# A new hand-listed order of the pinned stretch, with five chunks of batch 0 mixed in plain fp32 in place of three

## The chip, the cores and the metric

The kernel runs on one core of one Trainium2 chip. The metric is device microseconds (us) of one execution; the kernel before took 568.13 us, the median of three runs between 565.83 and 570.65. The profile shows one further execution.

## The reference, cut to what matters

Three layers run one after the other on 4 batches of 768 tokens with 384 channels (8 heads of 48):

```
state = alpha[t] * state + outer(k[t], v[t]);  y[t] = q[t] @ state          # gated linear attention, per head
theta = x @ w_theta;  zr = x*cos(theta);  zi = x*sin(theta)
y = w_tok_r @ zr + w_tok_i @ zi                                             # mix over all 768 tokens
u = x + y;  u = u + relu(u @ w_ch)
h = relu(u @ w_in);  c = conv3 over tokens(h);  out = (h * sigmoid(c)) @ w_out
```

All values are float32. The weights arrive as 64-bit words from which the kernel puts together the float32 numbers itself.

## The kernel before, in words

A *chunk* is 128 tokens; chunk numbers 0 to 23 run over four batches of six. For a chunk the attention part does this, each step under the name that the order list uses:

- `load`: SyncE (SP) fetches alpha (`a_t`), q and k (`qk_t`) and v. `hl` does it for the theta weights, `wl` for the twelve pieces of the token-mixing weights.
- `back`, `fore`, `mul`: VectorE (DVE) forms products of decays by a scan in either direction (L315, L329) and multiplies q and k by them (L344).
- `kps`, `sc`: TensorE (PE) transposes k (L364) and forms the scores; `pt0`, `pt1`: ScalarE (ACT) copies the scores' two halves out of PSUM (L379), and GpSimd (POOL) zeroes what lies above the diagonal (L380). `kt` is ACT's copy of the transposed k (L391).
- `y`, `kv`: PE multiplies the masked scores by v, adds q times the state that the chunk before left, and forms this chunk's addition to the state. `st`: DVE adds it (L446), and POOL multiplies by the decay in two instructions (L448). The next chunk's `y` needs both of them and both masks.
- `x`, `xt`, `u`: ACT copies y out, PE transposes it (L461), and ACT copies it to `u` (L466).

Then the second layer begins: `th` (PE, x times the theta weights `whole`), `int`, `frac`, `abs`, `sin` (ACT and DVE bring the angle into range and take sine and cosine), and `zm` (DVE, L514). For most chunks the product is split into a rounded high part (`tc`, ACT, L523) and a low rest (`tl`, DVE, L529), and `m0`, `m1`, `m2` mix it with the token weights, split in the same way (`lc` on ACT, L223; `ll` on DVE, L230), in three passes of the fast format: high by high, high by low, low by high. For the chunks listed in `PLAINS`, which exist in batch 0 alone, nothing is split: `zm` writes the operand and PE multiplies in plain fp32, which the profile records as two instructions for each matmul (`yps<-full,zh`). The two halves of the output tokens have a piece of token weights each, so an index of `m` is half times 6 plus chunk. `wo` decodes one piece of token weights on DVE in three instructions (L154, L155, L156), `wh` the theta weights, in a part of 768 columns and one of 384, each followed by a scaling on ACT (L288).

All of this for the chunks 0 to 13 and for the whole mixing of batch 0 stands in one string, `ORDER`. Its tokens are run from left to right, and `in_order` (L604) chains the instructions of each compute engine in just this sequence, so no engine can take a later instruction of the string while an earlier one waits. SP is not chained, but a later load waits behind an earlier one in its queue. `warm.n` puts in n matmuls on constants whose result nothing uses. Behind the string come the mixing of batches 1 to 3 and the last layer, where a scheduler sets the order. The token weights of the `PLAINS` chunks are split for the later batches: for the first half by `lc` and `ll` in the string, for the second half inside the loop over batch 1 if the string has not done it. The last chunk of `PLAINS` gets its low part by way of another buffer and one more copy on ACT (L234).

Of the kernel before, what the change touches and what calls it, by code (L numbers as in the profile page):

```python
# [37 lines left out]
STB = 2  # L38
NWARM = 13
WHOLE = 2  # L40
PLAINS = (0, 1, 3)
FINEY = 0
FINEK = 2 * NC
EARLY = 99
AHEAD = 2
ORDER = (
# [25 lines left out]
)  # L72
ENGINES = (mybir.EngineType.PE, mybir.EngineType.DVE, mybir.EngineType.Activation, mybir.EngineType.Pool)
MAGIC = 12582912.0
# [5 lines left out]
def tile_gated_linear_attention__then__spectral_moe__then__conv_gate(  # L80
# [53 lines left out]
    def body(top, slow):  # L134
# [50 lines left out]
        with ExitStack() as ph1:  # L185
# [12 lines left out]
            def tok_tile(h, dtype, name):  # L198
                return tok_ps[h].tile([P, 2, HALF], dtype, tag="w", name=name, bufs=2 * NC)


            def load_tok(h, c):
# [8 lines left out]
                nc.sync.dma_start(out=st[:, : 2 * n].bitcast(U32).rearrange("p (a n) -> p a n", a=2), in_=src)  # L211
                if c in PLAINS:
                    w = tok_tile(h, F32, "full").rearrange("p i t -> p (i t)")
# [11 lines left out]
            def tok_low(h, c):  # L225
                if slow:
                    return
                last = PLAINS and c == PLAINS[-1]
                lo = zf_p.tile([P, 2, DM], F32R, tag="zf", name="wlow") if last else tok_tile(h, F32R, "wtok")
# [240 lines left out]
            def t_mm(ci):  # L470
                b, c = divmod(ci, NC)
                xt = ub[b][:, :, c * P : (c + 1) * P]
                plain = ci in PLAINS and not slow
                zh = z_p.tile([P, 2, DM], F32 if plain else F32R, tag="zh", name="zh", bufs=ZH)
# [35 lines left out]
            def t_mul(ci):  # L510
                zh, th, z = ths[ci]
                plain = ci in PLAINS and not slow
                x = xs.pop(ci)
# [6 lines left out]
            def t_cast(ci):  # L520
                zh, th, z = ths[ci]
                if ci not in PLAINS or slow:
                    nc.scalar.copy(zh, z)  # L523

            def t_low(ci):
                zh, th, z = ths.pop(ci)
                if ci not in PLAINS or slow:
                    zl = z_p.tile([P, 2, DM], F32R, tag="zl", name="zl", bufs=NC)
# [418 lines left out]
```

## Time and profile before

| | |
|---|---|
| median of three runs | 568.13 us (565.83 to 570.65) |
| the profiled execution | 569.6 us, of which 567.9 us lie between the first and the last instruction |
| PE busy | 548.5 us (97%) |
| DVE busy | 451.2 us (79%) |
| ACT busy | 334.0 us (59%) |
| POOL busy | 90.9 us (16%) |
| mean granted TensorE clock | 0.989 of 2.4 GHz |

Matmuls overlap, and each one's record lasts longer than the pitch at which they follow each other. What PE needs for a run of equal matmuls is therefore read from start to start. PE counts as busy while a `warm` matmul runs, too, so that the busy share of the first stretch says little.

### The profile page before, as it was taken

How to read it: one execution, taken by the hardware profiler on the slowest of the kernel's cores; microseconds unless marked ns; L12 is line 12 of the kernel's file. 1: busy time of each engine (PE TensorE's matmuls, PEld its weight loads, DVE VectorE, ACT ScalarE, POOL GpSimd, SP SyncE). 2: the span in 40 equal slices, each digit the busy share in tenths (PEclk: the TensorE clock that was granted, in tenths of full speed). 3: DMA queues.
4: the chain of work that ended last, by engine and by line, in shares of the span. 5: the costliest groups of instructions: out<-in, count | busy, mean ns of one | idle time of the engine just before them, and what ended most of it. 6: DMA issues, size and time to landing. Idle time of an engine off the chain costs nothing.

```text
span 567.9 us, 13255 instructions
## 1 busy us (share of the span) xinstructions
PE 548.5 (97%) x5550; PEld 497.5 (88%) x5551; DVE 451.2 (79%) x680; ACT 334.0 (59%) x682; POOL 90.9 (16%) x99
## 2 busy tenths in 40 slices
PE   7879999999999999999999997999999999999996
PEld 4556778677998999899999996799999999999996
DVE  7995999999968775534757989887888888898780
ACT  4655673658736676435632436567667766676671
POOL 2573363333314102430000000000000000000000
PEclk9998999999999999999999999999999999999999
DMA  8664556553224301300024335200154342646001
GB/s 324 194 192 143 184 145 235 148 213 90 71 72 141 127 1 48 110 18 0 1 83 165 85 98 180 87 6 36 25 186 139 126 160 105 204 141 240 17 29 47
DMA packets 24995, 65.56 MB, mean 115 GB/s; under 512 B 2528, under 2 KB 8672, under 8 KB 24544
## 3 DMA queue, kind: packets, MB, share of 16 engines
q1 hardware_dynamic: 24928, 64.64, 34.6%
q8 instruction: 45, 0.74, 0.6%
q14 instruction: 22, 0.18, 0.1%
HBM read 59.92 MB, written 4.72 MB: 114 GB/s over the span
## 4 chain that ended last, share of the span: by engine, by line
PE 79%; DVE 11%; DMA 6%; POOL 2%; issue 1%; ACT 1%; SPq 0%; DVEq 0%; POOLq 0%
PE yps L99 22%; PE ops L99 18%; PE hps L99 16%; PE th L99 6%; PE y L99 5%; PE sc L99 4%; PE cps L99 3%; DMA stage<-in_w_out_dram 2%; PE kv L99 2%; DMA stage<-in_w_in_dram 2%; DVE stage L155 2%; PE xps L461 1%; DMA stage<-in_w_theta_dram 1%; DVE stage L156 1%; PE kps L364 1%
## 5 line engine op out<-in xcount | busy, mean ns | idle before, releaser
L99 PE MATMUL yps<-wtok,zh 128*128 128x384 f32 x504 | 133.7, 340 | 0.0
L99 PE MATMUL hps<-x,win 128*128 128x386 f32 x576 | 108.3, 340 | 0.0
L99 PE MATMUL ops<-wout,g 128*128 128x384 f32 x576 | 107.0, 337 | 0.0
L99 PEld LDWEIGHTS hps<-x,win 128*128 128x128 f32 x576 | 103.0, 190 | 0.5
L99 PEld LDWEIGHTS ops<-wout,g 128*128 128x128 f32 x576 | 101.6, 188 | 0.5
L99 PEld LDWEIGHTS yps<-wtok,zh 128*128 128x128 f32 x504 | 90.8, 188 | 2.4 <-ACT zh L523 0.3
L99 PE MATMUL yps<-wtok,zl 128*128 128x384 f32 x252 | 84.4, 335 | 0.0
L380 POOL TENSOR_SCALAR_AFFINE_SELECT pt<-pt 128x512 f32<-128x512 f32 x48 | 51.5, 1087 | 107.8 <-ACT pt L379 107.3
L99 PEld LDWEIGHTS yps<-wtok,zl 128*128 128x128 f32 x252 | 47.3, 188 | 0.1
L108 DVE TENSOR_TENSOR g<-cv,g 128x384 fp32r<-128x384 f32 x64 | 35.4, 555 | 12.1 <-ACT g L107 11.1
L99 PE MATMUL cps<-us,wch 128*128 128x512 f32 x162 | 41.3, 404 | 3.6 <-DVE u L714 1.9
L771 ACT ACTIVATE cv<-cv 128x384 f32<-128x384 f32 x64 | 33.1, 522 | 19.9 <-DVE cv L768 19.8
L772 DVE SCALAR_TENSOR_TENSOR cv<-cv,hh 128x384 f32<-128x384 f32 x64 | 35.2, 555 | 10.4 <-ACT cv L771 8.9
L315 DVE TENSOR_TENSOR_SCAN fbt<-a_t,onehot 128x516 f32<-128x516 f32 x24 | 30.3, 1261 | 14.6 <-ACT a_t L336 12.9
L765 DVE SCALAR_TENSOR_TENSOR cv<-hh,cw,cv 128x383 f32<-128x383 f32 (+1 forms) x64 | 38.8, 615 | 3.3 <-ACT cv L762 2.8
L762 ACT ACTIVATE cv<-hh,cw 128x384 f32<-128x384 f32 x64 | 38.6, 614 | 4.0 <-DVE g L108 3.8
L107 ACT CAST g<-cv 128x384 fp32r<-128x384 f32 x64 | 32.6, 510 | 13.3 <-DVE cv L772 12.0
L99 PEld LDWEIGHTS cps<-us,wch 128*128 128x128 f32 x162 | 30.6, 191 | 11.2 <-DVE u L714 2.4
L768 DVE SCALAR_TENSOR_TENSOR cv<-hh,cw,cv 128x384 f32<-128x384 f32 (+1 forms) x64 | 38.8, 615 | 1.0
L379 ACT COPY pt<-sc 128x512 f32<-128x512 f32 x48 | 26.8, 589 | 19.6 <-PE sc L99 11.3
L760 ACT ACTIVATE hh<-hps 128x386 f32<-128x386 f32 x64 | 31.5, 492 | 9.5 <-PE hps L99 9.3
L448 POOL TENSOR_TENSOR S<-tst,ftot 48x192 f32<-48x192 f32 x32 | 31.0, 969 | 37.2 <-DVE tst L446 30.9
(101 smaller groups left out, 847.9 us busy)
## 6 DMA issues: line engine op xcount, KB each, us to landing
qk_t<-in_qka_dram SPq DMA_DIRECT2D x24, 512.0 KB, 4.2
stage<-in_w_tok_dram SPq DMA_DIRECT2D x12, 768.0 KB, 4.7
top<-in_w_tok_dram SPq DMA_DIRECT2D x12, 768.0 KB, 4.4
a_t<-in_qka_dram SPq DMA_DIRECT2D x24, 260.0 KB, 2.8
v_t<-in_v_dram SPq DMA_DIRECT2D x24, 192.0 KB, 4.2
out_dram<-ob SPq DMA_DIRECT2D x24, 192.0 KB, 1.9
stage<-in_w_in_dram SPq DMA_DIRECT2D x4, 768.0 KB, 5.1
stage<-in_w_out_dram SPq DMA_DIRECT2D x4, 768.0 KB, 5.2
```

The lines of the kernel that those rows point to most:

```text
L99: nc.tensor.matmul(o, lhsT, rhs, start=start, stop=stop, skip_group_check=True)
L107: cast = nc.scalar.copy(hi, src)
L108: lo_eng.tensor_tensor(lo, src, hi.bitcast(F32), ALU.subtract)
L315: nc.vector.tensor_tensor_scan(bf[:, AW:0:-1], at[:, AW:0:-1], of[:, AW:0:-1], 0.0, ALU.mult, ALU.add)
L380: nc.gpsimd.affine_select(pt, pt, [[0, NP], [1, P]], ALU.is_ge, 0.0, base=0, channel_multiplier=-1)
L448: nc.gpsimd.tensor_tensor(Sn[r, :, e], tt[r, :, e], nft[r].unsqueeze(2).to_broadcast([D, NP, D]), ALU.mult)
L760: nc.scalar.activation(hh, ps[:, :HW], AF.Relu)
L762: nc.scalar.activation(cv, hh[:, o : o + HALF], AF.Copy, scale=cw[:, f, 1:2])
L765: nc.vector.scalar_tensor_tensor(cv[:, a:HALF], hh[:, o + a - 1 : o + HALF - 1], cw[:, f, 0:1], cv[:, a:HALF], ALU.mult, ALU.add)
L768: nc.vector.scalar_tensor_tensor(cv[:, 0:e], hh[:, o + 1 : o + 1 + e], cw[:, f, 2:3], cv[:, 0:e], ALU.mult, ALU.add)
L771: nc.scalar.activation(cv, cv, AF.Tanh, scale=0.5)
L772: nc.vector.scalar_tensor_tensor(cv, cv, 1.0, hh[:, o : o + HALF], ALU.add, ALU.mult)
```

## The change: five plain chunks and another order

`PLAINS` takes in five chunks of batch 0. The plain chunks need no `tc` and no `tl`, their mixing takes two recorded instructions for each plain matmul in place of three fast passes, and with chunk 4 as the last of the list, its low weights take the detour that chunk 3's took. In the string `ORDER` all tokens but a few stand elsewhere; the second half's weights are split in the string for chunk 5 alone and for the other five in the loop over batch 1. The number of `warm` matmuls goes from 35 to 33.

```diff
-PLAINS = (0, 1, 3)
+PLAINS = (0, 1, 2, 3, 4)
...
-    "back.0 fore.0 tot.0 sq.0 mul.0 kps.0 sc.0 back.1 hl.0 load.2 wl.2 load.3 load.4 wl.0 load.5 load.6 load.7 "
+    "back.0 fore.0 tot.0 sq.0 mul.0 kps.0 sc.0 back.1 fore.1 load.2 hl.0 load.3 wl.0 load.4 load.5 load.6 wl.2 "
```

PE at the first chunks: before its second `kps` and `sc` (of chunk 1) it had the first `y` and `kv`.

```order
 L644 MATMUL wps<-onehot 128x512
-L99 MATMUL y<-v_t,pt 32x48 x32
-L99 MATMUL kv<-v_t,kt 64x96 x8
-L644 LDWEIGHTS onehot
-L644 MATMUL wps<-onehot 128x512
 L644 LDWEIGHTS onehot
 L644 MATMUL wps<-onehot 128x512
 L364 MATMUL kps<-ident,qk_t 128x128 x4
 L99 MATMUL sc<-qk_t 128x128 x8
+L99 MATMUL y<-v_t,pt 32x48 x32
+L99 MATMUL kv<-v_t,kt 64x96 x8
```

The transposes and scores of chunk 1 now stand ahead of the output and the state of chunk 0.

DVE around the state of chunk 2 (`tst<-S_107,kv`), as it stood before:

```order
L446 TENSOR_TENSOR tst<-S_107,kv 112x384
L154 TENSOR_SCALAR full<-stage 128x768
L344 TENSOR_TENSOR qk_t<-qk_t,fbt 128x1024
L514 TENSOR_TENSOR zh<-x,zf 128x768
L230 TENSOR_TENSOR wtok<-stage,wtok 128x768
L155 SCALAR_TENSOR_TENSOR full<-stage,full 128x768
L156 SCALAR_TENSOR_TENSOR full<-stage,full 128x768
L499 SCALAR_TENSOR_TENSOR zf<-zf,th 128x384
```

The same place in the changed kernel, from the last part of the theta weights (`whole`, 384 columns) on:

```order
L156 SCALAR_TENSOR_TENSOR whole<-stage,whole 128x384
L329 SCALAR_TENSOR_TENSOR fbt<-a_t,starts 128x516
L499 SCALAR_TENSOR_TENSOR zf<-zf,th 128x384
L344 TENSOR_TENSOR qk_t<-qk_t,fbt 128x1024
L156 SCALAR_TENSOR_TENSOR full<-stage,full 128x768
L446 TENSOR_TENSOR tst<-S_107,kv 112x384
L514 TENSOR_TENSOR zh<-x,zf 128x768
L315 SCALAR_TENSOR_TENSOR fbt<-a_t,onehot 128x516
L319 RECIPROCAL starts<-fbt 128x4
L499 SCALAR_TENSOR_TENSOR zf<-zf,th 128x384
L329 SCALAR_TENSOR_TENSOR fbt<-a_t,starts 128x516
L344 TENSOR_TENSOR qk_t<-qk_t,fbt 128x1024
```

Behind the state's addition, five long instructions in a row (L344, L514, L230, L155, L156) have become two (L514 and the scan L315), then two short ones (L319, L499); the first `frac` (L499) now stands ahead of the product of chunk 3 (L344).

## Rows read from the trace of the kernel before

**Rows 1.** Windows: length, then busy us of PE, PEld, DVE, ACT, POOL; clock, DMA.

```profile
20.00:40.00 20.00, 15.70 (x224) 11.19 (x215) 19.83 (x26) 13.05 (x29) 12.10 (x7) 1.00 0.56 177
40.00:47.00 7.00, 5.98 (x115) 4.69 (x116) 2.74 (x5) 2.45 (x6) 3.20 (x4) 0.51 0.70 231
...
60.00:80.00 20.00, 19.73 (x380) 15.23 (x378) 19.63 (x22) 12.44 (x27) 6.15 (x6) 1.00 0.48 144
...
345.00:365.00 20.00, 16.40 (x71) 13.59 (x70) 18.70 (x33) 9.85 (x22) 0.00 (x0) 0.91 0.35 120
```

**Rows 2.** Timeline of PE, chunk 3 and on: start, us, instruction, [idle before].

```profile
40.37 0.87 PE L99 MATMUL y<-v_t,pt 128*32 128x48 f32 x32 [2.54 <-POOL pt L380]
41.88 0.87 PE L99 MATMUL y<-v_t,pt 128*32 128x48 f32 x32 [0.65 <-POOL pt L380]
42.53 1.50 PE L99 MATMUL y<-S,qk_t 128*32 128x96 f32 x32
43.96 1.55 PE L99 MATMUL kv<-v_t,kt 128*64 128x96 f32 x16
45.44 3.58 PE L99 MATMUL yps<-full,zh 128*128 128x384 f32 x8
48.86 0.49 PE L461 MATMUL xps<-ident,x 128*128 128x128 f32 x3
...
53.60 0.89 PE L99 MATMUL y<-v_t,pt 128*32 128x48 f32 x64
...
55.88 3.00 PE L99 MATMUL yps<-full,zh 128*128 128x384 f32 x8
```

**Rows 3.** Timeline of POOL: the states of chunks 2 to 4, the masks between.

```profile
32.96 5.68 POOL L448 TENSOR_TENSOR S<-tst,ftot 48x192 f32<-48x192 f32 x2 [3.87 <-DVE tst L446]
38.72 3.11 POOL L380 TENSOR_SCALAR_AFFINE_SELECT pt<-pt 128x512 f32<-128x512 f32 x2
...
46.27 3.33 POOL L448 TENSOR_TENSOR S<-tst,ftot 48x192 f32<-48x192 f32 x2 [3.62 <-ACT kt L391]
...
56.71 1.95 POOL L448 TENSOR_TENSOR S<-tst,ftot 48x192 f32<-48x192 f32 x2 [1.01 <-DVE tst L446]
```

**Rows 4.** Waits of DVE up to 145 us: total us, times, longest.

```profile
DVE tst L446 <- PE kv L99: 5.2, 3, 4.2
DVE zh L514 <- ACT zf L508: 2.2, 1, 2.2
```

**Rows 5.** Timeline of PE: fast passes, then plain matmuls.

```profile
119.71 0.51 PE L99 MATMUL yps<-wtok,zh 128*128 128x384 f32 x2
...
120.23 0.51 PE L99 MATMUL yps<-wtok,zh 128*128 128x384 f32 x2
...
120.75 2.74 PE L99 MATMUL yps<-full,zh 128*128 128x384 f32 x8
123.33 0.60 PE L364 MATMUL kps<-ident,qk_t 128*128 128x128 f32 x4
```

**Rows 6.** Groups of DVE up to 260 us: count, busy us, mean ns, idle before.

```profile
L529 DVE TENSOR_TENSOR zl<-zf,zh 128x768 fp32r<-128x768 f32 x15 | 15.2, 1014 | 2.5 <-ACT zh L523 2.5
```

**Rows 7.** Timeline of PE, the first chunks.

```profile
14.23 1.16 PE L99 MATMUL sc<-qk_t 48*128 48x128 f32 x16
...
20.24 0.88 PE L99 MATMUL kv<-v_t,kt 128*64 128x96 f32 x16
...
25.18 4.14 PE L99 MATMUL th<-whole,u 128*128 128x384 f32 x12
```

**Rows 8.** Timeline of DVE and of ACT: theta weights, and products of chunks 1 and 2.

```profile
10.86 0.56 DVE L154 TENSOR_SCALAR whole<-stage 128x768 uint32<-128x768 uint32 x1 [0.48 <-DMA stage<-in_w_theta_dram]
11.33 1.66 DVE L344 TENSOR_TENSOR qk_t<-qk_t,fbt 128x1024 f32<-128x1024 f32 x1
...
18.51 1.47 DVE L344 TENSOR_TENSOR qk_t<-qk_t,fbt 128x1024 f32<-128x1024 f32 x1
...
24.14 0.53 ACT L288 ACTIVATE whole<-whole 128x384 f32<-128x384 f32 x1
```

48 rows, old and new, of the table ORDER are left out of this document.

## The prediction

> **What bounds the kernel now.** I read the busy shares first, then windows, then PE's timeline in the windows that are not full. PE is busy for 97% of the span, and from 60 us on the windows show it full (19.73 of 20 us) with DVE close behind (19.63), both at the full clock [rows 1]. Only two stretches are not full: the first 47 us, and 345 to 365 us, in the last layer's loading, which the change leaves in place. So work added to PE counts in full, work taken from DVE or ACT counts only where PE waits for it, and the gain has to come from the first 47 us.
>
> The reader should see one event there. The masks of chunk 3 come late: PE stands idle 2.54 us before the first half of `y.3`, another 0.65 us before the second [rows 2]. POOL is late because its two decay instructions of chunk 2 took 5.68 us, from 32.96 to 38.64, and the two masks behind them 3.11 us [rows 3]; DVE in turn waited up to 4.2 us for `kv.3` [rows 4]. Behind the idle time the granted clock is 0.51 from 40 to 47 us, the lower level of 1.2 GHz [rows 1]. What that costs: from 40.37 to 45.44 PE did y.3 and kv.3, then eight plain instructions up to 48.86, 8.49 us in all. The same y and kv took 2.28 us one chunk later (53.60 to 55.88) [rows 2], eight plain instructions 2.58 us at full clock (120.75 to 123.33) [rows 5], together 4.86. Without the 0.65 us of waiting that leaves 3.0 us for the clock. The event costs 2.54 + 0.65 + 3.0 = 6.2 us.
>
> **The change, part by part.**
>
> *Two more plain chunks: +3.0 us on PE.* A plain matmul is two recorded instructions of 2.58/8 = 0.3225 us, so 0.645 us; a triple of fast passes takes 0.52 us (119.71 to 120.23) [rows 5]. Two chunks times two halves, three `m` and two operands are 24 of them: 24 x 0.125 = 3.0 us. Nothing hides it, since this work lies where PE is full. The change takes in exchange two `tl` of 1.01 us from DVE [rows 6] and two `tc` from ACT. I cost these at nothing: the full PE hides them. Equally at nothing: the two `lc`/`ll` pairs moved into the loop over batch 1, which have a whole half of mixing ahead of their first use, and the two fewer `warm` matmuls, which fill idle time.
>
> *The order of the first 40 us: -6.2 us at the end of `kv.3`.* I follow the new order by hand.
> - `mul.1` waited behind the first theta instruction (start 11.33); that one had waited 0.48 us for its DMA [rows 8]. Now `mul.1` can start at 10.4, ends near 12.0, and `sc.1` ends near 13.6 instead of 15.3 [rows 7]. `y.0` and `kv.0` follow (to 15.1), the state's copy and decay end near 17.5, `kv.1` near 19.7. Before it was 21.05 (start 20.24 and sixteen instructions of a pitch of about 0.05) [rows 7]: 1.3 us earlier.
> - The load of chunk 2's q and k now stands ahead of theta's in SP's queue: 512 KB at the pace of that time, 1.3 to 1.8 us. Theta's first part can be decoded from about 12.2 rather than 10.86. From there to the end of `mul.2` before were 9.1 us (10.86 to 19.98), 1.6 of them `mul.1` [rows 8], so `mul.2` ends near 19.7 and `sc.2` near 21.8 (before 25.18 [rows 7]).
> - `th.0` needs all of theta. Its last three decodings stand behind `back.3` and the state of chunk 1, end near 24.5, and ACT's scaling ends near 25.1; before, it began at 24.14 [rows 8] and `th.0` at 25.18 [rows 7]. So nothing is gained here: PE, early with its scores, **waits anew for about 3.3 us** (21.8 to 25.1). `frac.0` waits for `th.0` too, and DVE with it for 2 us, because `mul.3` is behind it.
> - `y.2` and `kv.2` follow to 29.7, `th.1`, `xt.2`, `kps.3` and `sc.3` to 33.5, the first plain matmuls and `th.2` to 36.8, `kps.4` to 37.2.
> - The state of chunk 2 goes to POOL near 31.2. Beside it DVE now runs one long product, one scan and two short instructions, where before five long ones stood in a row. The trace has no such mixture; the nearest pairs are 3.33 and 1.95 us, the worst 5.68 [rows 3]. I take 3.2, near the middle one, then 2.6 for the two masks: they are ready at 37.0, when PE arrives. `y.3` and `kv.3` end near 39.4, against 45.4 before (48.86 less 3.42 for eight slowed plain instructions) [rows 2].
>
> That is 6.0 us earlier. By then PE has done four plain instructions more (1.3 us) and the scores of chunk 4 (1.1 us) less: 6.2 us in work. Bounds: with a pair of 1.95 us nothing more is gained, since `kps.4` holds PE until 37.2; with 5.68 us the masks come at 39.5 and the gain is 3.9 us. Above that lies only the clock, a rival below.
>
> A rule against the row. POOL's two instructions took 5.68 us beside back-to-back DVE work, 1.95 us in the best pair [rows 3], so DVE held POOL up for 3.7 us over five DVE instructions. The Trainium skill, SBUF — State Buffer, section "SBUF: two separate sides", says that the two engines share one port pair as an exclusive lock, which whichever starts first keeps for its whole instruction while the other blocks. By that rule each POOL instruction would wait for at most one DVE instruction of about 1.0 us, the pair would end within 1.95 + 2 x 1.0 = 4.0 us, and the masks would come 0.6 us behind `kps.4` at worst rather than 2.3 us. The row is worse than the rule, so the range goes by the row.
>
> *Behind 40 us.* PE stays ahead only if DVE keeps up, as it is at 98% from 60 to 80 us [rows 1]. DVE regains its two waits of 4.2 and 2.2 us [rows 4] and saves 2.0 us of `tl`, against some 3 us of new waits (at `frac.0`, and for theta's data): 5.4 us, more than the 3.2 us that PE is to end ahead. So DVE does not take the gain back.
>
> **Sum:** 3.0 - 6.2 = -3.2 us. The profiled execution took 569.6 us, 1.5 us above the median of the three runs; it becomes 566.4, and against the median 568.13 this gives 564.9. I forecast **565.0 us**.
>
> **The rivals.**
> 1. *The clock falls at the new wait.* Before `th.0` PE is idle for 3.3 us, longer than the 2.54 us behind which it fell in the trace [rows 2]. For it: that length. Against: the 2.54 us came with 0.65 us more of waiting and little work between, here scores come before and one `warm` behind. It would slow th.0, y.2, kv.2 and th.1, 6 us of work, by as much as it did before, 3.0 us: -3.2 + 3.0 = -0.2, **568 us**. Chance 0.22.
> 2. *The starved state returns, slower than before.* POOL's pair of chunk 2 or 3 takes 5.68 us again [rows 3], because DVE, rid of its waits, runs long instructions without a gap. It decides from about 3.4 us on, when the masks come after `kps.4`. At 5.68 us, 2.3 us of the gain are lost, PE stands idle again and the clock falls with its 3.0 us: 3.0 - 6.2 + 2.3 + 3.0 = +2.1, **570.2 us**, and near 573 if it comes together with rival 1. For it: POOL's share is largest just there (12.10 of 20 us) [rows 1]; against: the shorter run of long DVE instructions beside the pair. Chance 0.16.
> 3. *DVE is the true bound of 60 to 145 us.* At 98% [rows 1], its small delays reach PE. Then the 2.0 us of `tl` [rows 6] come through as a gain as well, with about 0.6 us of the waits regained: -3.2 - 2.6 = -5.8, **562.3 us**. For it: both engines are full there. Against: PE's own row is full too. Chance 0.17.
> That the change does not do what it says is excluded by the order: the plain chunks and the moved scores stand there.
>
> **How the numbers follow.** The forecast has 0.45, its own range 562.5 to 567.5 (the pair of POOL, 1.3 us of theta's load, an error of a microsecond in a chain by hand). Eight times in ten needs rival 1, most of 3 and of 2: 560.5 to 571.0. One per cent, about what a measurement here tells from no change, is 5.7 us: below 562.4 lie a little over half of rival 3 and a tenth of the forecast, 0.16; above 573.8 the worst of rival 2 and what I have not seen, 0.06; the rest, 0.78, is within.
>
> **What would show it.** Right: no wait of PE for POOL above 0.5 us before `y.3`, `kv.3` ending near 39 us, `th.0` at about 25 us behind some 3 us without a wait for scores, 120 rows of plain matmuls, a full PE from 47 us on. Wrong: a clock of 0.5 anywhere between 20 and 50 us (rivals 1 or 2), POOL's decay pair above 4 us (2), a span shorter by 5 us with PE no earlier at `kv.3` (3); or a PE that waits in the loop over batch 1 for the five late splits, which I costed at nothing.

## The result, and the profile after

The changed kernel took 562.06 us, the median of eight runs (560.18 to 562.54); the kernel before, beside it on the same chip, 566.84 us (eight runs, 565.48 to 570.65). The ratio is 0.9902, with a 95% interval from 0.9876 to 0.9928: 4.8 us faster, just under one per cent. The forecast was 565.0 us, its range 560.5 to 571.0.

The two profiled executions differ by more, 569.6 against 560.2 us. The former lies 2.8 us above the median of its kernel, the latter 1.9 below. So the whole time is explained from medians, and the traces are used for places. The head of the page after:

```profile
span 558.5 us, 13194 instructions
...
PE 546.2 (98%) x5523; PEld 489.9 (88%) x5525; DVE 446.5 (80%) x678; ACT 333.1 (60%) x680; POOL 89.8 (16%) x99
...
PEclk9999999999999999999999999999999999999999
```

The granted clock is at nine tenths or more in every slice, and 1.00 in each of the windows below. The windows of [rows 1] again, with one more at 145 us (length, busy us of PE, PEld, DVE, ACT, POOL; then the clock and the DMA):

```profile
20.00:40.00 20.00, 19.27 (x346) 13.92 (x348) 17.91 (x24) 12.47 (x27) 7.82 (x9) 1.00 0.57 180
40.00:47.00 7.00, 7.00 (x46) 4.36 (x46) 6.86 (x9) 3.35 (x9) 6.65 (x4) 1.00 0.74 250
60.00:80.00 20.00, 20.00 (x276) 13.48 (x275) 17.43 (x23) 14.10 (x31) 6.62 (x7) 1.00 0.56 179
145.00:200.00 55.00, 55.00 (x801) 53.27 (x801) 43.29 (x55) 31.09 (x62) 12.66 (x16) 1.00 0.28 88
345.00:365.00 20.00, 19.20 (x91) 16.30 (x91) 19.31 (x41) 12.19 (x28) 0.00 (x0) 1.00 0.29 107
```

From 20 to 40 us PE was busy for 15.70 us before [rows 1] and now for 19.27; from 40 to 47 us, where the clock was 0.51, it is full at the full clock. DVE, busy for 19.63 us from 60 to 80, now has 17.43. And the last row has changed as well: PE was busy for 16.40 of 20 us in the last layer's loading, and is for 19.20. The prediction had said that this stretch stays as it is.

PE's timeline through the first chunks, which answers to [rows 2, 7] (start, us, instruction, idle time before it and who ended it):

```profile
12.53 1.16 PE L99 MATMUL sc<-qk_t 48*128 48x128 f32 x16
...
20.36 0.87 PE L99 MATMUL y<-S,qk_t 128*32 128x96 f32 x32 [1.63 <-POOL S L448]
21.16 0.88 PE L99 MATMUL kv<-v_t,kt 128*64 128x96 f32 x16
...
22.89 1.16 PE L99 MATMUL sc<-qk_t 48*128 48x128 f32 x16
23.98 2.33 PE L99 MATMUL th<-whole,u 128*128 128x384 f32 x6
26.63 1.14 PE L99 MATMUL y<-v_t,pt 128*32 128x48 f32 x64 [0.33 <-POOL pt L380]
...
36.49 0.60 PE L364 MATMUL kps<-ident,qk_t 128*128 128x128 f32 x4
37.02 0.89 PE L99 MATMUL y<-v_t,pt 128*32 128x48 f32 x64
37.72 0.84 PE L99 MATMUL y<-S,qk_t 128*32 128x96 f32 x32
38.49 0.88 PE L99 MATMUL kv<-v_t,kt 128*64 128x96 f32 x16
```

Chunk 3's output (37.02) has no idle time in front of it, and its `kv` ends at 39.3, against 45.44 before [rows 2]. The reason stands on POOL, the same instructions as in [rows 3]:

```profile
14.95 2.93 POOL L380 TENSOR_SCALAR_AFFINE_SELECT pt<-pt 128x512 f32<-128x512 f32 x2 [2.56 <-ACT pt L379]
17.84 2.46 POOL L448 TENSOR_TENSOR S<-S,ftot 48x192 f32<-48x192 f32 x2
...
30.13 2.74 POOL L448 TENSOR_TENSOR S<-tst,ftot 48x192 f32<-48x192 f32 x2 [2.96 <-DVE tst L446]
34.03 2.40 POOL L380 TENSOR_SCALAR_AFFINE_SELECT pt<-pt 128x512 f32<-128x512 f32 x2 [1.16 <-ACT pt L379]
40.20 4.12 POOL L448 TENSOR_TENSOR S<-tst,ftot 48x192 f32<-48x192 f32 x2 [3.76 <-ACT a_t L336]
```

The decay pair of chunk 2 takes 2.74 us in place of 5.68, and the masks of chunk 3 are ready at 36.4, before PE comes to them. What DVE does beside that pair:

```profile
29.90 0.94 DVE L514 TENSOR_TENSOR zh<-x,zf 128x768 f32<-128x768 f32 x1
30.77 1.22 DVE L315 TENSOR_TENSOR_SCAN fbt<-a_t,onehot 128x516 f32<-128x516 f32 x1
32.02 0.18 DVE L319 RECIPROCAL starts<-fbt 128x4 f32<-128x4 f32 x1
32.73 0.55 DVE L499 SCALAR_TENSOR_TENSOR zf<-zf,th 128x384 f32<-128x384 f32 x1 [0.53 <-ACT zf L494]
```

Two long instructions, then a gap of half a microsecond: POOL is through at 32.87. PE's waits in the loading part and the mixing of batch 0 (up to 150 us: total us, times, longest):

```profile
PE y L99 <- POOL S L448: 1.6, 1, 1.6
...
PE th L99 <- DVE fbt L315: 0.8, 1, 0.8
...
PE y L99 <- POOL pt L380: 0.3, 1, 0.3
```

The wait of about 3.3 us for the theta weights is not among them.

### The profile page after: what moved, and what is told of

Its sections match the earlier page's. It is cut to its first block, busy times and chain, and to the rows that moved or that the text cites. A ratio compares the mean times of both kernels' runs of the same rounds, so it can differ in the third digit from the quotient of the medians.

```text
span 558.5 us, 13194 instructions
## 1 busy us (share of the span) xinstructions
PE 546.2 (98%) x5523; PEld 489.9 (88%) x5525; DVE 446.5 (80%) x678; ACT 333.1 (60%) x680; POOL 89.8 (16%) x99
## 4 chain that ended last, share of the span: by engine, by line
PE 87%; DVE 7%; DMA 3%; ACT 1%; issue 1%; POOL 0%; DVEq 0%; ACTq 0%; POOLq 0%
PE yps L99 28%; PE ops L99 18%; PE hps L99 16%; PE th L99 7%; PE y L99 5%; PE cps L99 5%; PE sc L99 4%; PE kv L99 2%; DMA stage<-in_w_out_dram 2%; PE xps L461 1%; PE kps L364 1%; DVE fbt L315 1%; DMA stage<-in_w_tok_dram 1%; DVE stage L155 1%; DVE qk_t L344 0%
## 5 line engine op out<-in xcount | busy, mean ns | idle before, releaser
L99 PE MATMUL yps<-wtok,zh 128*128 128x384 f32 x456 | 120.8, 339 | 0.0
L99 PEld LDWEIGHTS yps<-wtok,zh 128*128 128x128 f32 x456 | 81.9, 188 | 1.7
L99 PE MATMUL yps<-wtok,zl 128*128 128x384 f32 x228 | 76.2, 335 | 0.0
L380 POOL TENSOR_SCALAR_AFFINE_SELECT pt<-pt 128x512 f32<-128x512 f32 x48 | 52.9, 1118 | 113.1 <-ACT pt L379 112.8
L99 PE MATMUL yps<-full,zh 128*128 128x384 f32 x120 | 43.0, 492 | 0.0
L99 PEld LDWEIGHTS yps<-wtok,zl 128*128 128x128 f32 x228 | 42.8, 188 | 0.1
L99 PE MATMUL cps<-us,wch 128*128 128x512 f32 x162 | 40.1, 396 | 0.8 <-ACT us L107 0.7
L315 DVE TENSOR_TENSOR_SCAN fbt<-a_t,onehot 128x516 f32<-128x516 f32 x24 | 29.8, 1241 | 11.4 <-ACT a_t L336 9.5
```

The lines of the kernel that those rows point to most:

```text
L99: nc.tensor.matmul(o, lhsT, rhs, start=start, stop=stop, skip_group_check=True)
L315: nc.vector.tensor_tensor_scan(bf[:, AW:0:-1], at[:, AW:0:-1], of[:, AW:0:-1], 0.0, ALU.mult, ALU.add)
L380: nc.gpsimd.affine_select(pt, pt, [[0, NP], [1, P]], ALU.is_ge, 0.0, base=0, channel_multiplier=-1)
```

## The experiments

Each experiment was timed in five rounds against the kernel before, on the same chip. In the diffs a line is a piece of `ORDER`. "Mixing's end" stands for the start of the first matmul of `cps`, the product with `w_ch`; it parts the time into a front part and the rest. Some mixing is left then: its last matmul starts 23.4 us later in either kernel (328.0 us before, 323.6 in the change), so the differences are the same at either mark. How long the last layer's first stage takes is read from the same range, first to last start. Mixing's end is where the range in these groups' rows begins (count; then min, median and max ns; then first to last start; the shapes behind), before and then after:

```profile
L99 PE MATMUL cps<-us,wch x162: 388/394/632, 304.6 to 471.8; 128*128 128x512 f32 x162
```

```profile
L99 PE MATMUL cps<-us,wch x162: 390/393/505, 300.2 to 462.5; 128*128 128x512 f32 x162
```

| kernel | median, us | ratio to before, 95% | mixing's end, us | first to last `cps`, us |
|---|---|---|---|---|
| before | 566.2 to 566.8 | 1 | 304.6 | 167.2 |
| the change | 562.06 | 0.9902 [0.9876, 0.9928] | 300.2 | 162.3 |
| e1, clock kept up | 563.31 | 0.9942 [0.9919, 0.9965] | 302.0 | 162.8 |
| e2, before + five plain | 567.32 | 1.0005 [0.9983, 1.0026] | 308.0 | 162.2 |
| e3, change + three plain | 573.95 | 1.0124 [1.0092, 1.0156] | 315.0 | 162.4 |
| e4, before + gap | 561.78 | 0.9915 [0.9887, 0.9943] | 300.3 | 163.6 |
| e5, change, late scores | 562.15 | 0.9906 [0.9875, 0.9937] | 301.3 | 162.2 |
| e6, change, gap closed | 562.23 | 0.9914 [0.9882, 0.9946] | 301.9 | 162.3 |
| e7, e4 + early scores | 561.51 | 0.9898 [0.9866, 0.9929] | 299.5 | 165.6 |
| e8, e4 + five plain | 565.27 | 0.9968 [0.9936, 1.0000] | 303.3 | 162.3 |
| e9, e7 + four plain | 565.78 | 0.9985 [0.9963, 1.0006] | 305.3 | 162.3 |
| e10, the change again | 560.73 | 0.9889 [0.9853, 0.9924] | 300.5 | 162.4 |
| e11, e7 again | 561.48 | 0.9912 [0.9882, 0.9943] | 300.7 | 163.7 |

The last two columns come from the one profiled execution of each. In two of these, before and e7, the clock fell near 350 us as well, which makes their last column longer. At mixing's end the two traces of the change (with e10) lie 0.3 us apart, those of e7 (with e11) 1.2 us, so that a difference of one microsecond in that column says little.

**e1: the old stall, with the clock kept up.** Twelve matmuls on constants run in the wait before chunk 3's output.

```diff
-abs.1 pt0.3 pt1.3 y.3 kv.3
+abs.1 pt0.3 pt1.3 warm.12 y.3 kv.3
```

> The kernel before, with twelve more matmuls on constants (warm) put between the scores of chunk 4 and y.3, where PE stood idle for 2.54 us; 12 x 0.216 = 2.6 us, so they fill the wait and nothing else changes. Theory A (the gain of the change is the wait for the state of chunk 2 and the halved clock behind it, less 3.0 us for two more plain chunks): the granted clock stays whole between 40 and 47 us and the time falls by about the 3.0 us that I put down to the clock, to a ratio near 0.995. Theory B (the gain lies in the last layer's loading, at 345 to 365 us, where the trace of the change has no drop of the clock): no change within 1 us. Theory C (the gain is DVE work saved by the plain chunks): no change.

Measured: 563.31 against 566.16 us, 2.9 us less. PE, POOL and the window from 40 to 47 us in its trace:

```profile
37.64 2.76 PE L644 MATMUL wps<-onehot 128*128 128x512 bf16 x12
40.34 0.55 PE L99 MATMUL y<-v_t,pt 128*32 128x48 f32 x32
...
42.89 0.88 PE L99 MATMUL kv<-v_t,kt 128*64 128x96 f32 x16
```

```profile
32.84 5.67 POOL L448 TENSOR_TENSOR S<-tst,ftot 48x192 f32<-48x192 f32 x2 [3.87 <-DVE tst L446]
```

```profile
40.00:47.00 7.00, 6.13 (x126) 4.20 (x125) 4.29 (x5) 2.73 (x7) 4.76 (x4) 1.00 0.78 262
```

POOL's pair is as long as before and `y.3` starts at the same time, 40.3. But `kv` now takes 0.88 us instead of 1.55, the granted clock is 1.00 from 40 to 47 us, and the kernel is faster. So the half clock alone was worth about 3 us, as worked out in the prediction, and idle PE time in front of it was what brought it on. The other executions agree: of the 58 of the kernel before that were timed beside the experiments, none has a mean clock above 0.997; of e1's eight, four have 0.999 or 1.000.

**e4: one gap in DVE's row, nothing else.** In the kernel before, the `ll.2` and `wo` steps that stood between the state of chunk 2 and the next `frac` go behind it.

```diff
-zm.0 ll.2 wo.0 wo.0 abs.1 pt0.3 pt1.3 y.3 kv.3 m0.0 int.2 sq.4 frac.2 m1.0
+zm.0 abs.1 pt0.3 pt1.3 y.3 kv.3 int.2 sq.4 frac.2 ll.2 wo.0 wo.0 m0.0 m1.0
```

> The kernel before with one move: on DVE the third frac (L499, which waits for its angle) stands ahead of the low weights of chunk 2 (L230) and of the two last decodings of the first piece (L155, L156), in place of behind them, so that DVE leaves a gap beside POOL's two state instructions of chunk 2. Three plain chunks, everything else in the order before. Theory A: POOL's pair of 5.68 us shrinks below 4 us, y.3 starts near 38 us in place of 40.4, the clock stays whole, and the time falls by 4 to 6 us, ratio 0.989 to 0.993. Theory B and theory C: no more than 1 us.

Measured: 561.78 us, 4.4 us less than before; mixing's end comes 4.3 us earlier. POOL, DVE and PE:

```profile
33.04 3.33 POOL L448 TENSOR_TENSOR S<-tst,ftot 48x192 f32<-48x192 f32 x2 [3.87 <-DVE tst L446]
36.44 1.22 POOL L380 TENSOR_SCALAR_AFFINE_SELECT pt<-pt 128x512 f32<-128x512 f32 x2
```

```profile
33.34 1.22 DVE L344 TENSOR_TENSOR qk_t<-qk_t,fbt 128x1024 f32<-128x1024 f32 x1
34.48 0.95 DVE L514 TENSOR_TENSOR zh<-x,zf 128x768 f32<-128x768 f32 x1
37.03 0.55 DVE L499 SCALAR_TENSOR_TENSOR zf<-zf,th 128x384 f32<-128x384 f32 x1 [1.60 <-ACT zf L494]
```

```profile
37.84 0.89 PE L99 MATMUL y<-v_t,pt 128*32 128x48 f32 x64
```

DVE now *waits* for 1.60 us (`frac` for ACT, from 35.43 on), and in that time POOL gets on: the pair takes 3.33 us, the masks 1.22, PE has no wait before `y.3`, and the clock is 1.00 from 40 to 47 us. This one move, with three plain chunks and everything else left in its place, gives nearly as much as the whole change.

**e2 and e8: the five plain chunks alone,** in the order of before and in that of e4. The two `lc`/`ll` pairs of chunks 2 and 4 move to the string's end, the second half's to the loop over batch 1.

```diff
-PLAINS = (0, 1, 3)
+PLAINS = (0, 1, 2, 3, 4)
...
-frac.1 st.2 lc.2 wo.0
+frac.1 st.2 wo.0
...
-sin.7 lc.8 tc.6 mul.11 ll.8 wo.9
+sin.7 tc.6 mul.11 wo.9
```

> The kernel before in its own order, with five plain chunks in place of three; the tokens for splitting the weights of chunks 2 and 4 are moved behind their last use or left to the loop over batch 1. Theory A: slower by 3.0 us (24 plain matmuls at 0.645 us in place of triples at 0.52), ratio near 1.005, since PE is full from 47 us on; a little more or less if the stall at 38 us moves. Theory B: slower or the same, with the difference in the last stage. Theory C: faster by 2 to 4 us, as DVE loses two subtractions of 1.01 us and two of the weights' splits from the stretch where both engines are full.

> e4 with five plain chunks: the cost of two more plain chunks without the stall and without the fall of the clock in the way. Theory A: 3.0 us slower than e4 (24 plain matmuls at 0.125 us more than a triple), ratio to before near 0.997. Theory C (the four long instructions that DVE loses come back to PE): 0 to 1.5 us slower than e4, ratio 0.991 to 0.994, as e2 against the kernel before (0.3 us by the ratio, 1.2 us by the medians).

Measured: with e2 mixing's end comes 3.4 us later, with e8 3.0 us later than e4's. The forecast was 3.0 for the 24 plain matmuls, but they do not make up this delay as it stands. Up to chunk 14's scores, behind the last plain matmul, PE takes the same steps in the same order in e4 and e8. Here are the scores of chunk 6, ahead of the first new plain matmul, and of chunk 14, in e4 and then in e8:

```profile
54.66 1.16 PE L99 MATMUL sc<-qk_t 48*128 48x128 f32 x16
...
141.24 1.16 PE L99 MATMUL sc<-qk_t 48*128 48x128 f32 x16
```

```profile
53.38 1.16 PE L99 MATMUL sc<-qk_t 48*128 48x128 f32 x16
...
142.42 1.16 PE L99 MATMUL sc<-qk_t 48*128 48x128 f32 x16
```

At the first mark e8 is 1.3 us early, at the second 1.2 us late: 2.5 us are lost between them, where the new plain matmuls stand, and another 1.8 behind the string. PE's waits between the marks come to 0.5 us in e4 and 0.3 in e8, so the matmuls themselves cost 2.7 us. Up to the first mark the two strings differ in `lc.2` and `ll.2` alone, which have gone from there. e2 does the same against before (58.5 against 59.6 us, then 147.1 against 145.9; waits of 0.3 us in before, none in e2: 2.6 us).

The stage from the first to the last `cps` got shorter at the same time, by 1.3 us from e4 to e8, so that the whole moved less: e2 took 567.32 us against 566.16, by its ratio no change. e8's twelve executions part into two groups: six with a mean granted clock of 0.998 to 1.000 took 561.2 to 564.0 us (median 563.1), six with 0.990 to 0.993 took 566.6 to 569.4 (567.5). Beside e4's 561.78 the former say +1.3 us, near the 3.0 less 1.3 of the traces. The latter are 4.4 us slower at the lower clock, so that the same program has a fall of the clock in some executions and not in others; the traced one belongs to the former, and where the clock falls in the others is not seen. And e8 waits in the loop over batch 1 (e4's row, then e8's):

```profile
145.00:200.00 55.00, 53.92 (x794) 52.11 (x793) 43.52 (x56) 30.94 (x62) 14.49 (x17) 1.00 0.27 88
```

```profile
145.00:200.00 55.00, 52.90 (x786) 50.76 (x786) 45.10 (x57) 32.82 (x63) 14.85 (x18) 1.00 0.27 88
```

PE is idle there for 2.1 us, in e4 for 1.1, in the change for none.

**e3: the changed order with three plain chunks.** `PLAINS` is put back; `tc`, `tl`, `lc` and `ll` of the two chunks come back into the string.

```diff
-PLAINS = (0, 1, 2, 3, 4)
+PLAINS = (0, 1, 3)
...
-wo.2 wo.2 m2.0 kps.5
+wo.2 wo.2 lc.2 ll.2 m2.0 kps.5
...
-kv.5 th.4 m2.2 m0.2
+kv.5 th.4 tc.2 tl.2 m2.2 m0.2
```

> The changed order, but with three plain chunks again: the casts and subtractions for chunks 2 and 4 and the splitting of their weights are put back at the first place behind their data. Theory A: faster than the change by up to 3.0 us, because PE does 24 triples in place of 24 plain matmuls, less what the eight long DVE instructions put back (about 7.7 us over the stretch) cost where PE waits for DVE; ratio to before 0.985 to 0.992. Theory C: slower than the change by 2 us or more, ratio 0.993 or above. Theory B: the same as the change, 0.990.

Measured: 573.95 us, some 12 us more than the change. PE has waits that the change does not have, of which the longest are

```profile
PE yps L99 <- ACT zh L523: 2.4, 1, 2.4
PE y L99 <- POOL pt L380: 2.2, 1, 2.2
```

and the clock fell to 0.50 at about 50, 91 and 125 us. PE waits for steps that I put back by hand (`zh`, L523, is a `tc`). So the run shows only that the changed order does not take them at these places; on the price of a plain chunk it says nothing.

**e5 and e7: the early scores.** e5 takes them out of the changed kernel; e7 puts them into e4, with `mul.1` and the masks' steps `pt0.1` and `pt1.1`. The diff is e5's.

```diff
-warm.9 kps.1 sc.1 y.0 kv.0 pt0.1
+warm.9 y.0 kv.0 kps.1 sc.1 pt0.1
```

> The changed kernel with the first output and state (y.0, kv.0) ahead of the transposes and scores of chunk 1 again, as before; nothing else moved. Theory A (stall of POOL behind the state of chunk 2): the scores of chunk 1 end 1.7 us later and the state of chunk 1 some 1 us later, but th.0 needs the theta weights, which are ready at 25.3 us in the trace of the change, so at most 1 us is lost: ratio to before 0.990 to 0.992. Rival (the early scores are what the gain rests on): 2 us or more slower than the change, 0.994 or above.

> e4 (the kernel before with a gap for POOL, three plain chunks) with the scores of chunk 1 ahead of the first output, and its masks ahead of the state of chunk 0, as the change has them. If the early scores are worth something by themselves, the state of chunk 1 is ready about 1 us earlier, th.0 follows by at most 0.5 us (it begins at 25.2 us, the theta weights are ready at 24.7): 0 to 1 us faster than e4, ratio to before 0.990 to 0.992. Rival (with two masks more ahead of the state on POOL, y.1 waits for the state as in the trace of the change, 1.6 us): as e4 or up to 1 us slower.

Measured: 562.15 us without them (the change has 562.06) and 561.51 with them (e4 has 561.78). Mixing's end moves by about 1 us either way, no more than between the two traces of e7, and the times by less than their intervals. In the change the scores come earlier, but PE then waits for 1.6 us at `y.1` for POOL's state; in e5 that wait is 0.7 us.

**e6: the gap closed in the changed kernel.** `frac.1` goes behind `mul.4`, so that DVE has long instructions in an almost unbroken row beside the pair.

```diff
-int.1 frac.1 fore.4 mul.4 wo.1 wo.1 th.2 kps.4 pt0.3 abs.1 pt1.3 y.3
+int.1 fore.4 mul.4 wo.1 wo.1 frac.1 th.2 kps.4 pt0.3 pt1.3 abs.1 y.3
```

> The changed kernel with the second frac (L499) behind the scan, the product and the two decodings that followed it (L329, L344, L154, L155), and abs.1 behind the second mask's copy on ACT, so that DVE runs without a gap beside POOL's two state instructions of chunk 2: the move of e4 undone in the other order. Theory A: the pair grows from 2.7 us to about 5, the masks of chunk 3 end after 38 us, PE waits before y.3 for 1 to 2 us, and with the clock falling 3 us more: slower than the change by 1.5 to 5 us, ratio to before 0.993 to 0.999. Rival (the changed order has enough other work for PE, and its gain does not rest on POOL): within 1 us of the change.

Measured: 562.23 us, no slower than the change. The pair grew to 3.65 us only:

```profile
29.86 3.65 POOL L448 TENSOR_TENSOR S<-tst,ftot 48x192 f32<-48x192 f32 x2 [2.96 <-DVE tst L446]
33.76 1.91 POOL L380 TENSOR_SCALAR_AFFINE_SELECT pt<-pt 128x512 f32<-128x512 f32 x2 [0.25 <-ACT pt L379]
```

The masks were ready at 35.7, ahead of `y.3` at 36.75. The expectation missed: this row, with no gap on DVE from 29.6 to 34.6 us, did not starve POOL as the one before had. So a full row of long instructions is not enough by itself, and the changed kernel does not hang on that one gap.

**e9: e7 with four plain chunks,** chunk 2 added. `lc.2` and `ll.2` move to the string's end, chunk 8's pair to the loop over batch 1.

```diff
-PLAINS = (0, 1, 3)
+PLAINS = (0, 1, 2, 3)
...
-ev.3 ll.0
+ev.3 lc.2 ll.2 ll.0
```

> e7 (three plain chunks, the gap for POOL, early scores) with chunk 2 plain as well: PE gets 12 plain matmuls for 12 triples, 1.5 us more, and DVE loses the low weights of chunk 2 beside the state (L230) and one tl. Theory A (plain chunks cost their PE time): 1.5 us slower than e7, ratio to before near 0.9925. Theory C in the form that e2 and e8 left (DVE's saved instructions give back 1.8 of 3.0 us for two chunks): chunk 2 is the one whose weights hold a stage buffer early, so most of the 1.8 us comes with it: within 0.5 us of e7, 0.9890 to 0.9905.

Measured: 565.78 us, a miss. PE waited once for 3.1 us for a low weight (`ll`, L230) that I had put late in the string, and the clock fell behind that, at 145.7 us. That is a wait of my making, and the whole time tells nothing of a plain chunk. The part ahead of it does: at chunk 6's scores e9 is 1.0 us ahead of e7 (53.2 against 54.2 us), at chunk 14's 0.2 us behind (141.0 against 140.8), so that 12 plain matmuls took 1.2 us for the 1.5 forecast. The second trace of e7 (e11: 54.2 and 141.7) gives 1.3 us once its 0.9 us of longer waits in between are taken off.

**e10 and e11: the change and e7 once more,** together, without an edit, to tell which is the better.

> The changed kernel once more, for another profile of the last layer and for its time beside e9 and e7 on one chip: 0.990 to before. If the clock's drop near 350 us in the trace of the kernel before is a matter of the single execution (how late one load of w_out lands) and not of the change, it may appear here as well, then with a span some 3 us longer.

> e7 once more, beside the change on the same chip: the sum of the stall (-4.7 us), of the early scores (-0.5 us) and no cost of plain chunks gives 0.989 to 0.991 to before; about 0.7 us below the change, which five rounds may not tell apart.

Measured: 560.73 and 561.48 us, with intervals that overlap by far. No version of these beats the change.

## Why the prediction was right, and where it was not

**Right: the stall, its cause and its price.** That this row of DVE's long instructions held up POOL's pair, that PE idled for it, and that the clock fell behind: e4 takes away the first link and all three go; e1 takes away the last alone and gets 2.9 us back for the predicted 3.0. The price of the whole event, 6.2 us, was too high as seen from mixing's end, where e4 gains 4.3: part of what PE is early at `kv.3` is given back behind it. The step "DVE does not take the gain back" holds for less than the whole.

**Right in size, but not by the sum at mixing's end: the price of two plain chunks.** +3.0 us was predicted, and +3.0 (e8 against e4) and +3.4 (e2 against before) stand at mixing's end. That agreement is partly chance. Between the two marks, where the matmuls are, they cost 2.7 us (e8) and 2.6 us (e2). Two things besides, which the prediction had not priced, nearly cancel: without `lc.2` and `ll.2` in their place PE is 1.3 and 1.1 us earlier at chunk 6's scores (1.0 in e9), and 1.8 and 2.2 us are lost behind the string, 1.0 of them in e8 as more idle time of PE in the loop over batch 1. The two `tl` saved on DVE lie between the marks; PE's waits got 0.2 to 0.3 us shorter there, so they brought next to nothing, as costed.

**Right at its end, wrong inside: the chain by hand.** `kv.3` was to end at 39.4 and ends at 39.3; POOL's pair was to take 3.2 us and takes 2.74, the masks 2.6 and 2.40. Between, two steps failed.
- `kv.1` was to end at 19.7 and ends at 22.0. With the scores early, chunk 1's masks reach POOL ahead of the state (2.93 us, then 2.46 for the pair), and PE waits for 1.6 us at `y.1`. I had written the state's end as near 17.5; POOL's queue, which I had not followed here, made it 20.3.
- The wait of 3.3 us before `th.0` did not appear. I had `th.0` need all of theta. It started at 23.98, before ACT's last scaling of theta ended at 25.3:

```profile
24.81 0.53 ACT L288 ACTIVATE whole<-whole 128x384 f32<-128x384 f32 x1 [1.18 <-DVE whole L156]
```

The first two of three parts of the contraction need only the 768 columns that were decoded earlier, so that PE had work until the last part came. The two errors cancelled; that `kv.3` came out at 39.3 is luck in that part. Nor was PE full from 47 us on, as the prediction had it: before a `th` at 57.3 us it waits 0.8 us for a scan of DVE.

**Wrong: "which the change leaves in place".** That step concerned the last layer's loading. Behind the string a scheduler sets the order, and with another string it set it otherwise there too. DVE's order in the last layer falls into two kinds over all kernels: one in before, e1, e4, e7 and e11, the other in the change, e2, e3, e5, e6, e8, e9 and e10. In the latter the splits of `x` and the second addition from `cps` stand ahead of the decoding of the next weights:

```
before                                         change
L714 u<-cps,u 128x512                          L714 u<-cps,u 128x512 x2
L108 win<-stage,win 128x3x256                  L108 win<-stage,win 128x3x256
L714 u<-cps,u 128x512                          L108 x<-u,x 128x386 x2
L108 x<-u,x 128x386                            L154 stage<-stage 128x768
L154 stage<-stage 128x768                      L714 u<-cps,u 128x512
```

PE's waits from 300 to 375 us, before and then after:

```profile
PE cps L99 <- DVE u L714: 1.9, 1, 1.9
PE cps L99 <- ACT us L107: 1.1, 2, 0.7
PE cps L99 <- DVE us L108: 0.6, 1, 0.6
```

```profile
PE cps L99 <- ACT us L107: 0.7, 1, 0.7
```

From the first to the last `cps` matmul the new order took 162.2 to 162.4 us in all eight executions, the old one 162.8, 163.6 and 163.7 in the three whose clock stayed up there: about 1.1 us more. In the two where the clock fell near 350 us it took 165.6 (e7) and 167.2 (before); none of the eight traces of the new order has such a fall. No run changes this order alone, so that it is the cause is concluded from the split and not shown by itself. That e2, with the early order of before, has the shorter last layer shows that this gain does not come from what the change does to the first 47 us.

**The sum.** Predicted: 3.0 - 6.2 = -3.2 us. Measured at mixing's end: 304.6 to 300.2, -4.4; of these -4.3 is the stall (e4), +3.0 what comes with the plain chunks in e8 (2.7 of it the matmuls), and the remaining -3.1 is what the changed order has better than e8. PE's idle 2.1 us in the loop over batch 1 are a part of the last; how much the changed order did and how much my late tokens in e8 spoiled was not separated. The last layer adds about -1.1, together -5.5, between the -4.8 of the first runs and the -5.9 of e10 (560.73 against 566.64). The term that was missing is the last layer's; the one mis-sized is the order's. A part of the distance is the starting point: the forecast counted from 568.13 us, the median of three runs, and from the 566.84 of eight the same sum gives 563.6, 1.6 us above what was measured.

**The rivals.** The clock did not fall at a new wait (1): the wait was not there, and behind the 1.6 us at `y.1` the clock stayed whole. The starved state did not hold PE up again (2), not even when e6 tried to bring it back. Its sign, a pair above 4 us, did appear: chunk 3's pair took 4.12 us in the change, but no wait of PE stood behind it. The third, DVE as the true bound, had the number nearly right (562.3 us), but not the cause: e8 takes the same `tl` from DVE, but in e4 PE waits for only 0.5 us between the marks, so that no more than that could come back there, and not 2.0; and what the change gained over the forecast lies partly in the last layer. The 1.3 us that `lc.2` and `ll.2` gave up to chunk 6 are a gain from ACT's and DVE's work in a place where PE was not full.

**The rule against the row.** Before and e1 show 5.68 and 5.67 us for POOL's pair beside five long DVE instructions, so one DVE instruction is not the most that POOL waits for. The Trainium skill, SBUF — State Buffer, section "SBUF: two separate sides", has whichever of the two engines starts first hold the port pair for its whole instruction while the other blocks; of VectorE's instructions it names those in a two-port mode and those with two inputs in SBUF. The five have two such inputs each, and so have four of the five in e6's row. The section does not say who comes next; that a POOL instruction waits for one DVE instruction at most was my addition, and the 4.0 us that I worked out with it is an estimate, which these two rows and the change's 4.12 us for chunk 3 exceed, while e4's 3.33, e6's 3.65 and the change's 2.74 us stay under it. Which DVE instructions let POOL in, and which do not, stays open: e6's row of long ones was nearly as tight.

## What to carry to other kernels

When an engine off the critical path is late, look at what its neighbour does beside it: here 1.6 us of idle time on DVE were worth 4.4 us of the whole, where five long DVE instructions without a gap had held POOL up. Another row without a gap did no harm (e6), so look at the trace of each. Follow every queue that a moved step passes, POOL's too, and ask of each matmul which part of its operand it needs first. Where a scheduler sets the order behind a hand-written stretch, compare the order there as well, before saying that a later stage stays as it is. And when a forecast of one term agrees at the end of a stage, read it also just before and just behind the work that it prices: here 3.0 us agreed at mixing's end, and 2.7 was the matmuls'.

## What the runs showed of the hardware

- A stall that left PE idle for 2.54 and 0.65 us was followed by half the clock; with twelve matmuls on constants in the first part it stayed whole (e1), and the kernel was 2.9 us faster.
- One program (e8) ran at a mean granted clock of 0.998 to 1.000 in six of twelve executions and at 0.990 to 0.993 in the other six, which were 4.4 us slower by their medians. Its median over all, 565.27 us, lies between the two groups, at a time that no execution took.
- POOL's decay pair, two instructions on the same sizes, took between 1.95 us [rows 3] and 5.68 us. It took 5.68 and 5.67 us beside five long DVE instructions without a gap and 3.33 us where DVE idled (e4), while DVE's long product beside the pair took 1.22 us in e4, no more than elsewhere (1.21 to 1.66 us in the kernel before).
